# Local and global attention with two feed-forward layers: the scheduler's durations, priorities and engines

## The chip, the cores and the metric

The kernel runs on one core of one Trainium2 chip. The metric is device time in microseconds (us). The kernel before took 911.58 us, the median of three runs (911.21 to 911.71).

The core has engines that run side by side, each with a queue of its own that it works off in order: TensorE (PE) multiplies matrices into PSUM; VectorE (DVE), ScalarE (ACT) and GpSimd (POOL) work element by element; SyncE (SP) issues all DMAs of this kernel. An engine waits at the head of its queue until what the next instruction needs is there, and nothing behind it may overtake.

## The reference

```python
# 4 batches, 8 heads, 512 local and 32 global tokens, head size 64
out_g = softmax(q_g @ k_all.T / 8) @ v_all          # global queries see all 544 keys
s_ll  = where(|i - j| <= 32, q_l @ k_l.T / 8, -1e9) # local queries see a window ...
s_lg  = q_l @ k_g.T / 8                             # ... and the 32 global keys
out_l = softmax([s_lg, s_ll]) @ [v_g, v_l]
x = [out_g, out_l] as 2176 tokens x 512
x = relu(x @ w1_in)**2 @ w1_out                     # 512 -> 2048 -> 512
return relu(x @ w2_in)**2 @ w2_out
```

## The kernel before

**Precision.** Every product of the layers and of the local scores is made of three matmuls: an operand is split into a rounded part (`xh`, `whi`, `gh`, `hk`, `hq`) and the rest (`xl`, `wlo`, `gl`, `lk`, `lq`), and high x high, low x high and high x low are summed in PSUM. So beside each copy that rounds there is a subtraction that makes the rest. The weights come as 64-bit numbers and are put together by four DVE instructions and a sign mask (L466 to L478), then split (L484, `minus("wl", ...)`).

**Attention.** 32 pairs of heads (8 units of 256 local queries, 4 pairs each) go through `pair`: load rk, rq, v; copy and subtract into hk, lk, hq, lq; 12 matmuls of scores into the two banks S0 and S1 (L314); the mask is added and the row minimum taken on DVE (L326); exp on ACT (L331); the sums' reciprocal on DVE (L336, L337); a multiplication of the scores `s` by it (`copy("nm", ...)`); transposes on PE (L349), a copy to `pt`, the product with v into O (L362), and the split of the result into xh (`copy("xh", ...)`) and xl (L373). Eight groups of global queries go through `glob` in the same way between the pairs.

**Layers.** The 2176 token columns are split into five blocks of 256, 512, 512, 512 and 384. Each layer is run in four waves of 512 hidden units; for each block a wave makes h (L509 to L511), on ACT r and gh (L519, L521), on DVE gf (L523), gl by `minus("gl", ...)`, and the product with the second weights (L534 to L536), added to y. A wave needs eight weight tiles: four for h, four for the product. There are 16 slots for them. Slots 8 to 15 lie over the attention's buffers, so weights 8 to 15 can be split only when the attention has ended; weights 0 to 7, of the first wave, come before. The first wave is worked off between the attention's instructions, as its blocks' columns become ready.

**What sets the order.** A planner at build time: every step is an `Op` with an engine, a duration and a priority. `Plan.order` simulates the engines: each takes, of the steps whose inputs are ready, the one with the lowest priority number. The order that comes out is written into the queues. So the durations in the `add` calls and the numbers in `CFG` decide which instruction stands where, and they are not known to the chip. The strings in `CFG` say in turn which engine makes a copy or subtraction (A, D, P for ACT, DVE, POOL): `ck` and `cq` copy hk and hq, `lo` is the subtraction lk, `nm` the multiplication of s, `ev` the copies pt, `xh` the copies xh, `wl` and `gl` the subtractions wlo and gl, `wa` the sign mask of a weight (L473 on DVE, L476 on ACT). `lead`, `lid` and `lmk` are priorities of loads, `glob` the places of the global groups, `moe`, `step`, `w0` and `w1` priorities of the first wave and of its weights.

Of the kernel before, what the change touches and what calls it, by code (L numbers as in the profile page):

```python
# [16 lines left out]
B, H, SL, SG, D = 4, 8, 512, 32, 64  # L17
# [6 lines left out]
WIN = 224  # L24
# [6 lines left out]
WAVES = 4  # L31
NSLOT = 16
CFG = {'EARLY': 8,
 'ck': 'AP',
 'cq': 'PDPD',
 'lo': 'PP',
 'nm': 'PPAD',
 'ev': 'AA',
 'yc': 'AA',
 'wl': 'PPDP',  # L40
 'gl': 'DDP',
 'xh': 'AAAA',
 'glob': [3, 11, 13, 17, 23, 27, 37, 39],
 'w0': 127.954,
 'w1': 1000.0,
 'moe': [122.595, 27.399, 55.448, 83.234, 128.881],
 'step': [0.2, 0.47, 0.409, 0.419, 0.141],
 'NK': 3,
 'NQ': 3,
 'wa': 'DDD',  # L50
 'lid': -23.363,
 'lmk': -11.49,
 'gbuf': '01',
 'lead': 30.038,
 'NM': 2,
 'NS': 3,
 'NPT': 4,
 'NV': 2,
 'NR': 2,
 'NG': 2,  # L60
# [121 lines left out]
def pe_r(n, m=128):  # L182
    return max(n + 32, 2 * m + 6) / 2400
# [3 lines left out]
def kernel(ctx: ExitStack, tc: tile.TileContext, kl, ql, vl, gk, gv, win, wout, msk, idn, out):  # L187
# [97 lines left out]
    def pair(j, prio):  # L285
        u, h2 = divmod(j, H // 2)
        kb, qb, mb, vb = j % NK, j % NQ, j % NM, j % NV
        A = ("arena",)
        q = [prio]

        def P():
            q[0] += 1e-3
            return q[0]

        K, Q, M, ML, HQ, LQ = ("rk", kb), ("rq", qb), ("hk", mb), ("lk", mb), ("hq", mb), ("lq", mb)
        lead = CFG["lead"]
        load(prio - lead, rk[kb], kl[j], 196608, A, (K,))
        load(prio - lead, rq[qb], ql[j], 131072, A, (Q,))
        load(prio - lead + 0.5, vt[vb], vl[j], 229376, A, (("v", vb),))
        copy("ck", P(), hk[mb], rk[kb], KW, A + (K,), (M,))  # L300
        copy("cq", P(), hq[mb], rq[qb], 256, A + (Q,), (HQ,), scalar=-0.125)
        add("DVE", dve(256), P(), lambda: nc.vector.scalar_tensor_tensor(
            out=lq[mb], in0=rq[qb], scalar=-0.125, in1=hq[mb].bitcast(F32),
            op0=ALU.mult, op1=ALU.subtract), A + (Q, HQ), (LQ,), lock=True)
        minus("lo", P(), lk[mb], rk[kb], hk[mb].bitcast(F32), KW, A + (K, M), (ML,))
        sk = [take("S", CFG["S"]) for _ in range(2)]

        def scores():
            for t in range(2):
                c, w = slice(128 * t, 128 * t + 128), slice(160 * t, 160 * t + WIN)  # L310
                for n, (a, b) in enumerate(((hq, hk), (lq, hk), (hq, lk))):
                    for e in range(2):
                        r = slice(64 * e, 64 * e + 64)
                        nc.tensor.matmul(out=bank[sk[e]][:, t * WIN:(t + 1) * WIN], lhsT=a[mb][r, c], rhs=b[mb][r, w],  # L314
                                         start=n == 0, stop=n == 2)

        add("PE", 12 * pe_r(WIN), P(), scores, A + (M, ML, HQ, LQ), tuple(sk))
        pbs = []
        ok = CFG["O"][j % len(CFG["O"])]
        for e in range(2):  # L320
# [13 lines left out]

            def tiny(sb=sb):
                nc.vector.tensor_scalar_add(out=sm[sb], in0=sm[sb], scalar1=1e-9)  # L336
                nc.vector.reciprocal(out=sm[sb], in_=sm[sb])  # L337

            add("DVE", 0.3, P(), tiny, A, (("sm", sb, 0), ("sm", sb, 1)), lock=True)
            for t in range(2):  # L340
                copy("nm", P(), st[sb][:, t, :], st[sb][:, t, :], WIN, A + (("sm", sb, t),), (("s", sb, t),),
                     scalar=sm[sb][:, t:t + 1])
            tk = take("PT", CFG["PT"])

            def trans(sb=sb, tk=tk):
                for t in range(2):
                    for c in range(2):
                        k = 2 * t + c
                        nc.tensor.transpose(bank[tk][0:112, 128 * k:128 * k + 128],  # L349
                                            st[sb][:, t, 112 * c:112 * c + 112], ident)  # L350

            add("PE", 0.44, P(), trans, A + (("s", sb, 0), ("s", sb, 1), "ident"), (tk,))
            pb = i % NPT
            copy("ev", P(), pt[pb][0:112, :], bank[tk][0:112, :], 512, A + (tk,), (("pt", pb),), psum=True)
            pbs.append(pb)

        def pv():
            for t in range(2):
                for c in range(2):
                    k = 2 * t + c  # L360
                    for e in range(2):
                        nc.tensor.matmul(out=bank[ok][64 * e:64 * e + 64, 128 * t:128 * t + 128],  # L362
                                         lhsT=vt[vb][:, 128 * k + 64 * e:128 * k + 64 * e + 64],
                                         rhs=pt[pbs[e]][0:112, 128 * k:128 * k + 128], start=c == 0, stop=c == 1)

        add("PE", 1.2, P(), pv, A + (("pt", pbs[0]), ("pt", pbs[1]), ("v", vb)), (ok,))
        b, c0 = UNIT_POS[u]
        split_out(b, [h2], xh[b][:, h2, c0:c0 + 256], xl[b][:, h2, c0:c0 + 256], ok, bank[ok][:, 0:256], 256, P)

# [7 lines left out]
    def glob(n, prio):  # L377
# [16 lines left out]
        for e in range(2):  # L394
# [4 lines left out]
                    nc.tensor.matmul(out=bank[sk][:, 0:272], lhsT=k[:, 1088 + 128 * pr:1216 + 128 * pr],  # L399
                                     rhs=k[:, S * pr + 272 * e:S * pr + 272 * e + 272], start=pr == 0, stop=pr == 1)  # L400

            add("PE", 0.92, P(), scores, A + (GK,), (sk,))
            add("DVE", 0.37, P(), lambda sk=sk, e=e: nc.vector.tensor_tensor_reduce(
                out=p[:, 272 * e:272 * e + 272], in0=bank[sk][:, 0:272], in1=zeros, op0=ALU.add, op1=ALU.max,
                scale=1.0, scalar=-3.0e38, accum_out=gmx[:, e:e + 1]), A + (sk, "masks"), (GP, "gmx"))
# [279 lines left out]
```

## Time and profile before

| | |
|---|---|
| median of three runs | 911.58 us |
| profiled execution | 911.63 us |
| its span, first to last instruction | 909.2 us |
| PE busy | 890.0 us (98%) |
| DVE busy | 570.4 us (63%) |
| ACT busy | 381.5 us (42%) |
| POOL busy | 214.9 us (24%) |
| mean granted TensorE clock | 0.998 of full |

The engines' shares are means over two very different parts. Up to about 203 us the attention runs, with the first wave's matmuls between; behind that PE has only the layers. Records of two matmuls overlap in time, since the engine starts one before the other has left it, and those of DVE and ACT do so a little; "busy" is the time that at least one record covers.

### The profile page before, as it was taken

How to read it: one execution, taken by the hardware profiler on the slowest of the kernel's cores; microseconds unless marked ns; L12 is line 12 of the kernel's file. 1: busy time of each engine (PE TensorE's matmuls, PEld its weight loads, DVE VectorE, ACT ScalarE, POOL GpSimd, SP SyncE). 2: the span in 40 equal slices, each digit the busy share in tenths (PEclk: the TensorE clock that was granted, in tenths of full speed). 3: DMA queues.
4: the chain of work that ended last, by engine and by line, in shares of the span. 5: the costliest groups of instructions: out<-in, count | busy, mean ns of one | idle time of the engine just before them, and what ended most of it. 6: DMA issues, size and time to landing. Idle time of an engine off the chain costs nothing.

```text
span 909.2 us, 14449 instructions
## 1 busy us (share of the span) xinstructions
PE 890.0 (98%) x5416; PEld 769.1 (85%) x5416; DVE 570.4 (63%) x1311; ACT 381.5 (42%) x885; POOL 214.9 (24%) x241
## 2 busy tenths in 40 slices
PE   5999999999999999999999999999999999999998
PEld 4778777778888988898889988998899889988888
DVE  5888999666557866755786686336754773333333
ACT  5887879683333322223333434343312332122221
POOL 4654556232112122202211221012111120010100
PEclk9999999999999999999999999999999999999999
DMA  8676644212221212200211022102210210001111
GB/s 293 202 239 214 212 133 145 76 31 65 75 70 56 78 53 70 70 24 18 75 50 45 1 70 70 47 1 70 69 47 1 70 47 1 1 1 47 47 47 58
DMA packets 28069, 67.92 MB, mean 75 GB/s; under 512 B 3168, under 2 KB 12512, under 8 KB 28000
## 3 DMA queue, kind: packets, MB, share of 16 engines
q1 hardware_dynamic: 28000, 67.01, 23.1%
q8 instruction: 42, 0.69, 0.3%
q14 instruction: 27, 0.22, 0.1%
HBM read 62.54 MB, written 4.46 MB: 74 GB/s over the span
## 4 chain that ended last, share of the span: by engine, by line
PE 90%; DVE 5%; ACT 2%; DMA 1%; issue 1%; SPq 0%; POOL 0%; DVEq 0%; POOLq 0%; ACTq 0%
PE h L509 8%; PE h L511 7%; PE h L510 7%; PE S L511 6%; PE S L509 6%; PE S L510 6%; PE PT L536 6%; PE PT L534 6%; PE PT L535 6%; PE Y L534 4%; PE Y L536 4%; PE Y L535 4%; PE O L534 3%; PE O L536 3%; PE O L535 3%; PE O L362 2%
## 5 line engine op out<-in xcount | busy, mean ns | idle before, releaser
L221 POOL TENSOR_TENSOR gl<-gf,gh 128x512 fp32r<-128x512 f32 (+2 forms) x53 | 63.1, 1191 | 377.0 <-DVE gf L523 326.9
L519 ACT ACTIVATE r<-h 128x512 f32<-128x512 f32 (+2 forms) x88 | 47.0, 534 | 227.7 <-PE h L511 213.9
L509 PE MATMUL h<-xh,whi 128*128 128x512 f32 (+2 forms) x352 | 129.5, 368 | 1.2 <-DVE gf L523 1.1
L511 PE MATMUL h<-xh,wlo 128*128 128x512 f32 (+2 forms) x352 | 126.4, 359 | 0.9 <-POOL wlo L221 0.9
L510 PE MATMUL h<-xl,whi 128*128 128x512 f32 (+2 forms) x352 | 126.4, 359 | 0.0
L221 POOL TENSOR_TENSOR wlo<-wt,whi 128x512 fp32r<-128x512 f32 x48 | 63.9, 1332 | 217.6 <-ACT whi L484 217.6
L511 PE MATMUL S<-xh,wlo 128*128 128x512 f32 (+2 forms) x288 | 102.8, 357 | 0.0
L510 PE MATMUL S<-xl,whi 128*128 128x512 f32 (+2 forms) x288 | 102.8, 357 | 0.0
L534 PE MATMUL PT<-gh,whi 128*128 128x512 f32 (+2 forms) x288 | 102.8, 357 | 0.0
L509 PE MATMUL S<-xh,whi 128*128 128x512 f32 (+2 forms) x288 | 102.8, 357 | 0.0
L536 PE MATMUL PT<-gh,wlo 128*128 128x512 f32 (+2 forms) x288 | 102.7, 357 | 0.0
L535 PE MATMUL PT<-gl,whi 128*128 128x512 f32 (+2 forms) x288 | 102.7, 357 | 0.0
L521 ACT ACTIVATE gh<-r 128x512 fp32r<-128x512 f32 (+2 forms) x160 | 90.7, 567 | 19.2 <-PE O L536 10.4
L523 DVE SCALAR_TENSOR_TENSOR gf<-h,r 128x512 f32<-128x512 f32 (+2 forms) x88 | 53.5, 608 | 71.6 <-ACT r L519 71.1
L466 DVE TENSOR_SCALAR wt<-wraw 128x512 uint32<-128x512 uint32 x64 | 31.2, 488 | 77.5 <-DMA wraw<-wout 38.8
L484 ACT ACTIVATE whi<-wt 128x512 fp32r<-128x512 f32 x64 | 40.1, 628 | 90.5 <-DVE wt L478 90.5
L534 PE MATMUL Y<-gh,whi 128*128 128x512 f32 (+2 forms) x208 | 76.3, 367 | 0.0
L509 PEld LDWEIGHTS h<-xh,whi 128*128 128x128 f32 x352 | 66.7, 189 | 10.8 <-DVE gf L523 1.6
L523 DVE SCALAR_TENSOR_TENSOR gf<-S,r 128x512 f32<-128x512 f32 (+2 forms) x72 | 43.7, 606 | 50.7 <-ACT r L519 50.4
L536 PE MATMUL Y<-gh,wlo 128*128 128x512 f32 (+2 forms) x208 | 74.9, 360 | 0.3 <-DVE sm L336 0.3
L535 PE MATMUL Y<-gl,whi 128*128 128x512 f32 (+2 forms) x208 | 74.7, 359 | 0.0
L511 PEld LDWEIGHTS h<-xh,wlo 128*128 128x128 f32 x352 | 66.5, 189 | 9.6 <-POOL wlo L221 1.1
(81 smaller groups left out, 1886.5 us busy)
## 6 DMA issues: line engine op xcount, KB each, us to landing
wraw<-win SPq DMA_DIRECT2D x32, 512.0 KB, 3.6
wraw<-wout SPq DMA_DIRECT2D x32, 512.0 KB, 3.5
v<-vl SPq DMA_DIRECT2D x32, 224.0 KB, 3.3
rk<-kl SPq DMA_DIRECT2D x32, 192.0 KB, 3.2
y<-gk SPq DMA_DIRECT2D x8, 672.0 KB, 4.2
y<-gv SPq DMA_DIRECT2D x8, 640.0 KB, 6.1
rq<-ql SPq DMA_DIRECT2D x32, 128.0 KB, 2.9
out<-y SPq DMA_DIRECT2D x12, 256.0 KB, 2.4
```

The source lines that it names most:

```text
L221: add("Pool", 0.25 + 0.0021 * n, prio, lambda: nc.gpsimd.tensor_tensor(out=get(out_), in0=a, in1=get(b), op=ALU.subtract), reads, writes)
L466: add("DVE", dve(512, True), P(), lambda: nc.vector.tensor_scalar(out=t, in0=high, scalar1=3, scalar2=0x3FFFFFF8, op0=ALU.logical_shift_le ...
L484: nc.scalar.activation(out=whi[slot], in_=tf, func=AF.Copy)
L509: nc.tensor.matmul(out=hp, lhsT=hi, rhs=xh[b][:, k, :], start=k == 0, stop=False)
L510: nc.tensor.matmul(out=hp, lhsT=hi, rhs=xl[b][:, k, :], start=False, stop=False)
L511: nc.tensor.matmul(out=hp, lhsT=lo, rhs=xh[b][:, k, :], start=False, stop=k == KD - 1)
L519: add("Activation", act(nb), P(), lambda r=r, hp=hp: nc.scalar.activation(out=r, in_=hp, func=AF.Relu), (hk,), (("r", ri),))
L521: add("Activation", act(nb) + 0.04, P(), lambda r=r, a=a: nc.scalar.activation(out=a, in_=r, func=AF.Square), (("r", ri),), (("gh", f),))
L523: add("DVE", dve(nb), P(), lambda r=r, hp=hp, gf=gf: nc.vector.scalar_tensor_tensor(out=gf, in0=hp, scalar=0.0, in1=r, op0=ALU.max, op1=AL ...
L534: nc.tensor.matmul(out=o, lhsT=hi, rhs=gh[f][:, 0:nb], start=f == 0, stop=False)
L535: nc.tensor.matmul(out=o, lhsT=hi, rhs=gl[f][:, 0:nb], start=False, stop=False)
L536: nc.tensor.matmul(out=o, lhsT=lo, rhs=gh[f][:, 0:nb], start=False, stop=f == 3)
```

## The change

New durations for six kinds of PE steps in the `add` calls; new engines for copies, subtractions, multiplications and sign masks; new priorities and places; one more buffer `pt` (five, not four). No instruction's shape changes and no matmul is added or removed.

```diff
- 'ck': 'AP',
- 'cq': 'PDPD',
- 'lo': 'PP',
- 'nm': 'PPAD',
+ 'ck': 'PPP',
+ 'cq': 'P',
+ 'lo': 'D',
+ 'nm': 'AD',
...
- 'wl': 'PPDP',
- 'gl': 'DDP',
- 'xh': 'AAAA',
- 'glob': [3, 11, 13, 17, 23, 27, 37, 39],
+ 'wl': 'DDPP',
+ 'gl': 'D',
+ 'xh': 'AADA',
+ 'glob': [5, 5, 13, 17, 19, 27, 31, 37],
...
- 'wa': 'DDD',
- 'lid': -23.363,
+ 'wa': 'DAA',
+ 'lid': -317.614,
...
- 'lead': 30.038,
+ 'lead': 14.017,
...
- 'NPT': 4,
+ 'NPT': 5,
...
-        add("PE", 12 * pe_r(WIN), P(), scores, A + (M, ML, HQ, LQ), tuple(sk))
+        add("PE", 0.86, P(), scores, A + (M, ML, HQ, LQ), tuple(sk))
...
-            add("PE", 0.44, P(), trans, A + (("s", sb, 0), ("s", sb, 1), "ident"), (tk,))
+            add("PE", 0.468, P(), trans, A + (("s", sb, 0), ("s", sb, 1), "ident"), (tk,))
...
-        add("PE", 1.2, P(), pv, A + (("pt", pbs[0]), ("pt", pbs[1]), ("v", vb)), (ok,))
+        add("PE", 1.03, P(), pv, A + (("pt", pbs[0]), ("pt", pbs[1]), ("v", vb)), (ok,))
```

(`12 * pe_r(WIN)` is 1.28. The other three durations are of the global groups and change by up to 0.04.)

The SP queue at its start, before (rk, rq and v are one pair's keys, queries and values, ident the unit matrix of the transposes, masks the mask table):

```order
L678 UNCONDITIONAL_BRANCH
L282 DMA rk0_110<-kl 128x384
L282 DMA rq0_113<-ql 128x256
L282 DMA v0_131<-vl 112x512
L282 DMA rk1_111<-kl 128x384
L282 DMA rq1_114<-ql 128x256
L282 DMA v1_132<-vl 112x512
L282 DMA rk2_112<-kl 128x384
L282 DMA rq2_115<-ql 128x256
L282 DMA ident_142<-idn 128x128
L282 DMA masks_141<-msk 128x672
```

The same queue at its start now:

```order
L678 UNCONDITIONAL_BRANCH
L282 DMA ident_143<-idn 128x128
L282 DMA rk0_110<-kl 128x384
L282 DMA rq0_113<-ql 128x256
L282 DMA v0_132<-vl 112x512
L282 DMA rk1_111<-kl 128x384
L282 DMA rq1_114<-ql 128x256
L282 DMA v1_133<-vl 112x512
L282 DMA masks_142<-msk 128x672
```

Ident moved from ninth to first place, the masks from tenth to eighth, and the third pair's rk and rq behind them.

The POOL queue from the third pair on, before (hk and hq are copies, lk a subtraction, s a multiplication):

```order
L211 TENSOR_SCALAR hq0_120<-rq2_115 128x256
L221 TENSOR_TENSOR lk0_118<-rk2_112,hk0_116 128x384
L211 TENSOR_SCALAR s0_124<-s0_124,sm0_136 128x224 x2
L211 TENSOR_SCALAR hk1_117<-rk0_110 128x384
L221 TENSOR_TENSOR lk1_119<-rk0_110,hk1_117 128x384
L211 TENSOR_SCALAR s2_126<-s2_126,sm2_138 128x224 x2
```

The POOL queue from the third pair on now:

```order
L211 TENSOR_SCALAR hk0_116<-rk2_112 128x384
L211 TENSOR_SCALAR hq0_120<-rq2_115 128x256
L211 TENSOR_SCALAR hk1_117<-rk0_110 128x384
L211 TENSOR_SCALAR hq1_121<-rq0_113 128x256
L211 TENSOR_SCALAR hk0_116<-rk1_111 128x384
L211 TENSOR_SCALAR hq0_120<-rq1_114 128x256
```

The subtractions lk and the multiplications s have left POOL; all copies hk and hq are there.

The DVE queue from lq of pair 8 (the ninth) on, before (L403 is a global group's row maximum):

```order
L302 SCALAR_TENSOR_TENSOR lq0_122<-rq2_115,hq0_120 128x256
L336 TENSOR_SCALAR sm0_136<-sm0_136 128x2
L337 RECIPROCAL sm0_136<-sm0_136 128x2
L523 SCALAR_TENSOR_TENSOR gf0_89<-h0_143,r0_87 128x256
L373 TENSOR_TENSOR xl1_70<-O0_150,xh1_65 128x256
L336 TENSOR_SCALAR sm1_137<-sm1_137 128x2
L337 RECIPROCAL sm1_137<-sm1_137 128x2
L403 ISA y3_77,gmx_139<-S0_146,masks_141 128x272
L403 ISA gmx_139 128x1
L208 TENSOR_SCALAR s1_125<-s1_125,sm1_137 128x224
```

The DVE queue from lq of the same pair on now:

```order
L302 SCALAR_TENSOR_TENSOR lq0_122<-rq2_115,hq0_120 128x256
L218 TENSOR_TENSOR lk0_118<-rk2_112,hk0_116 128x384
L336 TENSOR_SCALAR sm0_137<-sm0_137 128x2
L337 RECIPROCAL sm0_137<-sm0_137 128x2
L403 ISA y3_77,gmx_140<-S0_147,masks_142 128x272
L403 ISA gmx_140 128x1
L208 TENSOR_SCALAR s0_124<-s0_124,sm0_137 128x224
L336 TENSOR_SCALAR sm1_138<-sm1_138 128x2
L337 RECIPROCAL sm1_138<-sm1_138 128x2
L403 ISA y3_77,gmx_140<-S1_148,masks_142 128x272
L403 ISA gmx_140 128x1
L208 TENSOR_SCALAR s1_125<-s1_125,sm1_138 128x224
```

The subtraction lk now stands behind lq on DVE, and each of the pair's two heads has one multiplication of s there; before, a pair had one in all.

## Rows read from the trace of the kernel before

**Rows 1.** The page's part 1: engine, busy time, share, instructions.

```profile
span 909.2 us, 14449 instructions
PE 890.0 (98%) x5416; PEld 769.1 (85%) x5416; DVE 570.4 (63%) x1311; ACT 381.5 (42%) x885; POOL 214.9 (24%) x241
```

**Rows 2.** Busy time by stretches: PE, PEld, DVE, ACT, POOL; clock, DMA share, GB/s.

```profile
0.00:9.77 9.77, 1.97 (x12) 1.43 (x12) 2.60 (x3) 2.33 (x3) 4.34 (x10) 1.00 0.80 239
9.77:162.00 152.23, 144.37 (x1484) 116.85 (x1485) 135.43 (x535) 126.02 (x388) 82.50 (x119) 0.99 0.62 200
20.00:40.00 20.00, 17.71 (x201) 13.70 (x198) 18.39 (x78) 16.87 (x56) 12.73 (x18) 1.00 0.64 206
...
120.00:140.00 20.00, 18.73 (x229) 14.77 (x227) 19.25 (x76) 16.41 (x51) 11.34 (x15) 1.00 0.43 131
140.00:160.00 20.00, 18.33 (x173) 15.27 (x173) 18.68 (x67) 18.31 (x55) 12.21 (x17) 1.00 0.45 140
162.00:202.70 40.70, 40.70 (x329) 32.13 (x327) 24.97 (x102) 31.06 (x89) 13.63 (x22) 1.00 0.20 58
202.70:905.60 702.90, 702.90 (x3596) 618.65 (x3594) 406.81 (x671) 222.12 (x405) 114.39 (x92) 1.00 0.15 46
```

**Rows 3.** Timeline of PE in the steady part: start, duration, engine, line, instruction.

```profile
241.05 0.39 PE L509 MATMUL h<-xh,whi 128*128 128x512 f32 x1
241.28 0.39 PE L510 MATMUL h<-xl,whi 128*128 128x512 f32 x1
```

**Rows 4.** Timeline of DVE and POOL near the start.

```profile
3.92 1.00 POOL L221 TENSOR_TENSOR lk<-rk,hk 128x384 fp32r<-128x384 f32 x1
3.99 1.21 DVE L302 SCALAR_TENSOR_TENSOR lq<-rq,hq 128x256 fp32r<-128x256 f32 x1 [3.99 <-POOL hq L211]
...
9.77 0.39 DVE L326 CUSTOM_DVE_ANT_0 s<-S,masks 128x224 f32<-128x224 f32 x1 [1.66 <-DMA masks<-msk]
...
11.02 0.42 DVE L302 SCALAR_TENSOR_TENSOR lq<-rq,hq 128x256 fp32r<-128x256 f32 x1
...
11.36 0.16 DVE L336 TENSOR_SCALAR sm<-sm 128x2 f32<-128x2 f32 x1
...
12.61 0.34 DVE L208 TENSOR_SCALAR s<-s,sm 128x224 f32<-128x224 f32 x1
...
27.24 1.29 POOL L211 TENSOR_SCALAR s<-s,sm 128x224 f32<-128x224 f32 x2 [0.39 <-DVE sm L337]
...
27.34 0.62 DVE L302 SCALAR_TENSOR_TENSOR lq<-rq,hq 128x256 fp32r<-128x256 f32 x1
```

**Rows 5.** Timeline of pair 24's product and of its low part on DVE.

```profile
159.42 1.09 PE L362 MATMUL O<-pt,v 112*64 112x128 f32 x16
...
161.55 0.42 DVE L373 TENSOR_TENSOR xl<-O,xh 128x256 fp32r<-128x256 f32 x1
```

**Rows 6.** Groups by line: count, busy us, mean ns, idle before and releasers.

```profile
L221 POOL TENSOR_TENSOR lk<-rk,hk 128x384 fp32r<-128x384 f32 x32 | 33.9, 1060 | 2.1 <-ACT hk L203 1.0
L211 POOL TENSOR_SCALAR s<-s,sm 128x224 f32<-128x224 f32 x64 | 33.0, 528 | 37.3 <-DVE sm L337 13.7 <-ACT s L331 11.5 <-ACT pt L203 11.5
L302 DVE SCALAR_TENSOR_TENSOR lq<-rq,hq 128x256 fp32r<-128x256 f32 x32 | 19.6, 619 | 4.0 <-POOL hq L211 4.0
L336 DVE TENSOR_SCALAR sm<-sm 128x2 f32<-128x2 f32 x64 | 15.2, 237 | 8.9 <-ACT s L331 8.3
L208 DVE TENSOR_SCALAR s<-s,sm 128x224 f32<-128x224 f32 x32 | 14.9, 464 | 0.2
L218 DVE TENSOR_TENSOR gl<-gf,gh 128x384 fp32r<-128x384 f32 x21 | 11.7, 557 | 2.3 <-ACT gh L521 0.4
L208 DVE TENSOR_SCALAR hq<-rq 128x256 fp32r<-128x256 f32 x16 | 9.1, 571 | 1.5 <-DMA rq<-ql 1.5
```

**Rows 7.** Timeline of DVE: last step (L478) of weights 10 and 15.

```profile
208.50 0.69 DVE L478 SCALAR_TENSOR_TENSOR wt<-wraw,wt 128x512 f32<-128x512 f32 x1
...
244.35 0.69 DVE L478 SCALAR_TENSOR_TENSOR wt<-wraw,wt 128x512 f32<-128x512 f32 x1
```

More of the change, by code (lines that the diff above doesn't have):

```diff
@@ L33 @@
 CFG = {'EARLY': 8,
- 'ck': 'AP',
- 'cq': 'PDPD',
- 'lo': 'PP',
- 'nm': 'PPAD',
- 'ev': 'AA',
- 'yc': 'AA',
- 'wl': 'PPDP',
- 'gl': 'DDP',
- 'xh': 'AAAA',
- 'glob': [3, 11, 13, 17, 23, 27, 37, 39],
[L44 to L47, printed above, removed]
+ 'ck': 'PPP',
+ 'cq': 'P',
+ 'lo': 'D',
+ 'nm': 'AD',
+ 'ev': 'A',
+ 'yc': 'AA',
+ 'wl': 'DDPP',
+ 'gl': 'D',
+ 'xh': 'AADA',
+ 'glob': [5, 5, 13, 17, 19, 27, 31, 37],
+ 'w0': -1.361,
+ 'w1': 684422.049,
+ 'moe': [341.089, 23.225, 54.691, -112.195, -211.616],
+ 'step': [0.2638, 0.5671, 0.1425, 0.013, 0.2305],
  'NK': 3,
  'NQ': 3,
- 'wa': 'DDD',
- 'lid': -23.363,
+ 'wa': 'DAA',
+ 'lid': -317.614,
  'lmk': -11.49,
  'gbuf': '01',
- 'lead': 30.038,
+ 'lead': 14.017,
  'NM': 2,
  'NS': 3,
- 'NPT': 4,
+ 'NPT': 5,
  'NV': 2,
@@ L400, in scores @@
                                      rhs=k[:, S * pr + 272 * e:S * pr + 272 * e + 272], start=pr == 0, stop=pr == 1)
-            add("PE", 0.92, P(), scores, A + (GK,), (sk,))
+            add("PE", 0.96, P(), scores, A + (GK,), (sk,))
             add("DVE", 0.37, P(), lambda sk=sk, e=e: nc.vector.tensor_tensor_reduce(
@@ L425, in trans @@
                 nc.tensor.transpose(bank[t1][:, 128 * c:128 * c + 128], p[:, 128 * c:128 * c + 128], ident)
-        add("PE", 0.44, P(), trans, A + (GP, "ident"), (t1,))
+        add("PE", 0.49, P(), trans, A + (GP, "ident"), (t1,))
         copy("ev", P(), kt[:, 0:512], bank[t1], 512, A + (t1,), (GK,), psum=True)
-        add("PE", 0.11, P(), lambda: nc.tensor.transpose(bank[t2][0:32, 0:128], p[:, 512:544], ident),
+        add("PE", 0.15, P(), lambda: nc.tensor.transpose(bank[t2][0:32, 0:128], p[:, 512:544], ident),
             A + (GP, "ident"), (t2,))
@@ L441, in pv @@
                             rhs=kt[0:kc, 128 * c + 32 * j:128 * c + 32 * j + 32], start=c == 0, stop=c == 4)
-        add("PE", 1.61, P(), pv, A + (GK, GV), (ok,))
+        add("PE", 1.645, P(), pv, A + (GK, GV), (ok,))
         c0 = 256 + 32 * bb
```

## The prediction

> **What bounds the kernel now.** I read first the page's head: of a span of 909.2 us the TensorE (PE) counts as busy in 890.0 [rows 1]. So at most 19.2 us of idle shows, which makes the next question where it lies. The table by stretches answers [rows 2]: from 202.7 us, where the attention's last matmul has ended, to 905.6 PE is busy in 702.90 of 702.9 us, and behind that comes only the 3.6 us in which the last columns are added and stored. All visible idle but that lies before 162 us, 7.8 us up to 9.77 and 7.9 between 9.77 and 162; from 162 to 202.7 PE shows none.
>
> "Busy" hides more. In the steady part a 128x512 matmul is recorded with 0.39 us while the next one starts 0.23 us later [rows 3]; records overlap, so a matmul that is 0.15 us late leaves no idle in the table. The steady part has no such lateness (its matmuls follow each other at 0.23), and a new order can give nothing there: VectorE (DVE) is busy in 406.8 of its 702.9 us. What it can change is the first 202.7 us.
>
> There the reader should look at DVE. In the stretches in which PE shows idle, 20 to 40, 120 to 140 and 140 to 160, DVE is busy 18.39, 19.25 and 18.68 us of 20, a mean of 93.9%; over 9.77 to 162 it is 135.43 of 152.23, or 89.0% [rows 2]. ScalarE (ACT) has 126.0 and GpSimd (POOL) 82.5 in the same 152. So DVE comes last where PE falls back, with ACT close by.
>
> DVE itself waits for POOL inside its records. At 3.92 POOL begins a subtraction of 1.00 us, and the DVE instruction that begins at 3.99 takes 1.21; the same instruction with POOL idle takes 0.42 [rows 4]. A short POOL instruction holds it less: beside the two multiplications from 27.24 on it takes 0.62.
>
> And the first 9.77 us are a wait for the mask table: the first mask instruction on DVE starts there, released by that DMA, and scores of the next pair wait for it [rows 4].
>
> **The change part by part.** *The planner's durations* (scores 1.28 to 0.86 us of plan time, transposes, products) move no time by themselves: the matmuls are the same ones, and the chip doesn't know the plan. All effect comes through the new order and the new engines.
>
> *The start.* The SP queue now issues ident first and the masks eighth instead of tenth. Ahead of the masks stand 1.18 MB instead of 1.51 MB. At the 239 GB/s of the first 9.77 us [rows 2] the 0.33 MB are worth 1.4 us; in a queue with nothing else to do it could be as little as nothing, if the masks' own transfer sets the time. I take 1.1 us: masks at 8.7 in place of 9.77. The first pair's chunks arrive one issue later, which costs nothing as long as the masks come after its scores.
>
> *DVE's ledger up to the low part of pair 24's output* (L373; the 25th of 32 pairs, and the place where before has its worst stretch behind it). Counted in the program order of both, with durations less the overlap of 0.08 that records there show (one of 0.42 whose successor starts 0.34 later) [rows 4]:
> 28 subtractions lk come from POOL, at 0.48 each by the 0.557 of DVE's other 128x384 subtraction [rows 6]: +13.4. 27 more multiplications of s, at 0.34 - 0.08 [rows 4]: +7.0. 14 copies hq go to POOL, at the same price: -3.6. Eight copies xh from PSUM, five of 256 columns at 0.34 and three small ones: +2.1. Three more 128x512 subtractions at 0.64 and one of 256 columns: +2.3. One gf more: +0.6. Five sign masks L473 go to ACT: -1.7. Two more weight instructions stand ahead of this place: +1.3. Sum +21.4 us.
>
> *Against that, what POOL no longer holds.* The means of DVE's records against the unheld ones [rows 4] give what POOL costs it now: L302 (619 - 420 ns) x 32 = 6.4 us, L208 s (464 - 340) x 32 = 4.0, L336 (237 - 160) x 64 = 4.9, L208 hq (571 - 340) x 16 = 3.7 [rows 6]; 19.0 over 32 pairs, so 15 up to pair 24. POOL loses 28 subtractions of 1.06 us and 52 multiplications of 0.53, and gains 28 copies of about half a microsecond: its busy time up to there falls from 82.5 to some 39 us. In proportion DVE would still be held for 7 us; as what is left is short, and long ones hold longer, I take 5 (ends: 2, and 15 if nothing gets better). Relief 10 us.
>
> DVE's busy time to that place becomes 135.4 + 21.4 - 10 = 146.8 us. *ACT* gets 27 multiplications and six sign-masks and loses 14 hk and 8 xh copies: 11 instructions at its mean of 0.32 us, +4 on 126 of 152; it doesn't become the bound.
>
> *What PE gets for it.* Up to the product O of pair 24 the attention matmuls are the same in both orders, but after has 36 more 128x512 matmuls of the first layer ahead of it: at 0.227 [rows 3] 8.2 us of work already done. Before, that product ends at 159.42 + 1.09 = 160.5, and xl, its low part on DVE, 1.5 us later [rows 5].
>
> The step that decides is how full DVE is. I take the mean of the three stretches in which it came last, 93.9%: PE had reserve there and DVE none, and with the longer ledger DVE should come last nearly throughout. Then 146.8 / 0.939 = 156.4; from the masks at 8.7 that ends at 165.1, the product 1.5 earlier at 163.6. Before would have needed until 160.5 + 8.2 = 168.7 for as much work. Gain 5.1 us. At 89.0%, the mean over the whole stretch, the same sum ends 3.4 us later than before; at the best stretch's 96.3% it gains 9.0.
>
> *Behind pair 24* seven pairs are left in either order, where PE is full in 162 to 202.7 [rows 2]; I take no gain and no loss, with 2 us to either side. *The weights at the end of the attention* lose cover: weights 8 to 15 are written over the attention's buffers, so they start when its last product is done. In before the first matmul of weight 10 follows 44.5 us of PE work later, that of weight 15 77.8; in after 29.8 and 47.5. Weights 10 to 15 are finished on DVE at intervals of (244.35 - 208.50) / 5 = 7.2 us [rows 7], and weight 10's low part is there 8 us after the last product. So 15 is ready at 8 + 5 x 7.2 = 44, 3.5 us before it is needed. Hidden; the cover is used up when the interval grows by 0.7 us, to 7.9, and what it grows beyond that PE waits five times over.
>
> *The steady part*: DVE takes over 53 subtractions gl from POOL and gives two of three L473 to ACT. DVE at 58% covers it.
>
> The profiled execution took 911.63 us, its span and 2.4 around it, within 0.1 of the median of the three timed ones. 911.63 - 5.1 = 906.5.
>
> **The rivals.** *DVE is no better packed than now.* At 89.0% the attention reaches the same point 3.4 us later: 915.0. It decides from 90.9% downward, where 146.8 us take 161.5, as long as before. For it: outside the three stretches DVE was busy (135.43 - 56.32) / (152.23 - 60) = 86% and PE still came late now and then, so both can wait for each other in chains, while the queues run in order; more of a pair's chain (lk, then lq, the masks, the sums, half the multiplications) now sits in one queue. Against it: where PE waited for DVE it was over 91% each time, and two hops to POOL leave each pair's chain.
>
> *POOL holds DVE nearly as before.* The two multiplications at 27.24 held the DVE instruction as well, 0.62 against 0.42 [rows 4], so short copies do hold; and DVE runs more instructions that can be held. Of these (subtractions, multiplications, L302 and the weight chain in SBUF) after has about 1.3 times as many up to pair 24. 15 x 39 / 82.5 x 1.3 = 9 us of holding stay; DVE has 151 us, 160.9 at 93.9%, and the gain shrinks to 0.7: 910.9. The Trainium skill, "GPSIMD Engine Reference", Key points, has the rule: GpSimd's SBUF interfaces are VectorE's too, and it contends with DVE instructions that have two SBUF inputs or run in a 2-port mode. By it every lk and s that moves to DVE is one more that can be held; rows 4 agree in kind. The rule gives no price, and the sum of my forecast stands without it.
>
> *DVE is packed as in its best stretch*, since its queue nearly always holds ready work: 96.3%, 902.6; with holding at its lower end of 2 us 900.
>
> **How the numbers follow.** Forecast 906.5 with 0.42, its own range 903 to 909.5; better packed 0.25; held nearly as before 0.13; no better packed 0.20. The first two are faster by over 0.2%, that is 1.8 us, about what a measurement of this kernel can tell from no change: 0.67. Held is within it: 0.13. The last is slower: 0.20. The range goes from 899.5, the best packing with the low end of holding and half a microsecond, to 915, the no-better-packed case; the end without any relief (15 us of holding: 917) is left out.
>
> **What would show it.** Right: the first mask instruction at about 8.7; POOL busy near 40 us up to pair 24; L302's mean near 0.45; xl of pair 24 ending near 165 with DVE at 93% or more since the masks; the attention's last product, with 23.5 us more of the first layer ahead of it, ending near 202.7 + 23.5 - 5 = 221; 0.23 from matmul to matmul behind it. Wrong: xl of pair 24 at 170 or later with DVE under 90%, or with L302 still near 0.6; or PE idle behind the last product before weights 14 and 15.

## The result, and the profile after

The changed kernel took 904.38 us, the median of 4 runs (903.92 to 904.77), against 911.64 us for the kernel before beside it (4 runs, 911.21 to 913.55): a ratio of 0.9916 [0.9899, 0.9933]. It is faster by 7.3 us. The forecast was 906.5, faster, with a range of 899.5 to 915.

The page's head of the kernel after answers to [rows 1]. The profiled execution took 904.31 us, 1.8 of them around the span:

```profile
span 902.5 us, 14362 instructions
PE 888.0 (98%) x5416; PEld 765.8 (85%) x5416; DVE 577.3 (64%) x1396; ACT 405.2 (45%) x933; POOL 80.7 (9%) x108
```

POOL's 214.9 us have shrunk to 80.7; DVE's total has grown by 6.9 us only, though it runs 85 instructions more. The table by stretches, with the columns of [rows 2], cut at the first mask instruction, at the low part of pair 24 and at the attention's last product:

```profile
0.00:9.12 9.12, 1.96 (x12) 1.43 (x12) 2.06 (x4) 1.28 (x1) 2.38 (x8) 1.00 0.75 211
9.12:162.80 153.68, 149.81 (x1517) 120.97 (x1518) 142.91 (x586) 131.37 (x404) 36.78 (x64) 1.00 0.65 204
20.00:40.00 20.00, 19.83 (x236) 16.49 (x235) 19.10 (x85) 17.75 (x55) 5.08 (x8) 1.00 0.76 238
...
60.00:80.00 20.00, 19.87 (x236) 15.86 (x235) 19.12 (x85) 16.38 (x53) 6.44 (x11) 1.00 0.76 237
...
120.00:140.00 20.00, 19.16 (x219) 16.45 (x219) 17.62 (x75) 17.11 (x55) 5.84 (x10) 1.00 0.48 146
140.00:160.00 20.00, 19.28 (x154) 15.19 (x154) 18.85 (x69) 17.41 (x52) 2.96 (x6) 1.00 0.37 108
...
162.80:219.70 56.90, 56.90 (x404) 45.20 (x402) 29.31 (x114) 35.95 (x98) 3.55 (x8) 1.00 0.12 31
219.70:898.90 679.20, 679.20 (x3488) 598.22 (x3486) 402.52 (x693) 236.65 (x431) 38.04 (x28) 1.00 0.15 48
```

Where the kernel before had PE busy for 17.71, 18.73 and 18.33 us of 20 [rows 2], it is now busy for 19.83, 19.16 and 19.28. Behind the attention nothing has changed in kind: 679.20 busy of 679.20.

Busy time hides lateness, so I also took each matmul's start to the next start, less the usual step of its kind, and added these up. The numbers are how late PE is at a time, in us:

| at | 20 us | 40 | 80 | 120 | 160 | 220 | 890 |
|---|---|---|---|---|---|---|---|
| before | 12.9 | 17.6 | 22.7 | 24.8 | 31.7 | 34.2 | 34.9 |
| after | 14.8 | 15.7 | 18.9 | 21.3 | 24.9 | 27.6 | 28.2 |

The difference at the end is the span's 6.7 us. It is made between 20 and 40 us (4.7 lost before, 0.9 now), between 40 and 80 (5.1 and 3.2) and between 120 and 160 (6.9 and 3.6). In the second of these before loses some 1.7 us from 64 to 67.5 us at the lower of TensorE's two clock levels (the rows are in the last section):

```profile
60.00:80.00 20.00, 18.37 (x181) 15.39 (x182) 16.57 (x70) 15.00 (x46) 10.22 (x14) 0.91 0.70 222
```

The columns are those above; the mean granted clock is 0.91 here and 1.00 in the same stretch after. It isn't this execution alone: of the 70 runs of before beside the experiments, 53 have a mean granted clock of 0.998 or less over the whole run (median 912.2 us) and 17 have 0.999 or 1.0 (median 910.2), while all four runs of after have 0.999 or 1.0. So some 1.7 to 2 of the 7.3 us go with the clock.

The groups by line of the kernel after (count, busy us, mean ns, idle before) answer to [rows 6]:

```profile
L208 DVE TENSOR_SCALAR s<-s,sm 128x224 f32<-128x224 f32 x64 | 22.4, 351 | 0.4
L218 DVE TENSOR_TENSOR lk<-rk,hk 128x384 fp32r<-128x384 f32 x32 | 18.0, 563 | 6.5 <-POOL hk L211 6.5
L302 DVE SCALAR_TENSOR_TENSOR lq<-rq,hq 128x256 fp32r<-128x256 f32 x32 | 14.9, 466 | 0.5 <-POOL hq L211 0.5
L336 DVE TENSOR_SCALAR sm<-sm 128x2 f32<-128x2 f32 x64 | 13.2, 207 | 3.4 <-ACT s L331 3.0
```

The same instructions are shorter: L302 466 ns for 619, the multiplication L208 351 for 464, L336 207 for 237.

### The profile page after: what moved, and what is told of

Same layout as the page of the kernel before. It is cut to its first block, busy times and chain, and to the rows that moved or that the text cites. A ratio compares the mean times of both kernels' runs of the same rounds, so it can differ in the third digit from the quotient of the medians.

```text
span 902.5 us, 14362 instructions
## 1 busy us (share of the span) xinstructions
PE 888.0 (98%) x5416; PEld 765.8 (85%) x5416; DVE 577.3 (64%) x1396; ACT 405.2 (45%) x933; POOL 80.7 (9%) x108
## 4 chain that ended last, share of the span: by engine, by line
PE 92%; DVE 4%; ACT 2%; DMA 2%; issue 0%; SPq 0%; ACTq 0%
PE h L509 8%; PE h L510 7%; PE h L511 7%; PE S L510 6%; PE S L509 6%; PE S L511 6%; PE PT L534 6%; PE PT L536 6%; PE PT L535 6%; PE Y L534 5%; PE Y L536 4%; PE Y L535 4%; PE O L534 3%; PE O L535 3%; PE O L536 3%; PE O L362 3%
## 5 line engine op out<-in xcount | busy, mean ns | idle before, releaser
L218 DVE TENSOR_TENSOR gl<-gf,gh 128x512 fp32r<-128x512 f32 (+2 forms) x160 | 99.5, 623 | 21.5 <-ACT gh L521 10.4
L536 PE MATMUL PT<-gh,wlo 128*128 128x512 f32 (+2 forms) x288 | 102.6, 356 | 0.0
L535 PE MATMUL PT<-gl,whi 128*128 128x512 f32 (+2 forms) x288 | 102.6, 356 | 0.0
L221 POOL TENSOR_TENSOR wlo<-wt,whi 128x512 fp32r<-128x512 f32 x32 | 43.6, 1364 | 521.5 <-ACT whi L484 521.5
L536 PE MATMUL Y<-gh,wlo 128*128 128x512 f32 (+2 forms) x208 | 74.6, 359 | 0.0
L535 PE MATMUL Y<-gl,whi 128*128 128x512 f32 (+2 forms) x208 | 74.6, 359 | 0.0
L510 PEld LDWEIGHTS h<-xl,whi 128*128 128x128 f32 x352 | 66.5, 189 | 7.8 <-DVE xl L373 0.2
L547 DVE TENSOR_TENSOR y<-y,Y 128x512 f32<-128x512 f32 (+2 forms) x30 | 18.2, 606 | 84.3 <-PE Y L536 84.2
L519 ACT ACTIVATE r<-S 128x512 f32<-128x512 f32 (+2 forms) x72 | 38.4, 533 | 67.8 <-PE S L511 65.2
```

What stands on the lines that cost most here:

```text
L218: add("DVE", dve(n), prio, lambda: nc.vector.tensor_tensor(out=get(out_), in0=a, in1=get(b), op=ALU.subtract), reads, writes, lock=True)
L221: add("Pool", 0.25 + 0.0021 * n, prio, lambda: nc.gpsimd.tensor_tensor(out=get(out_), in0=a, in1=get(b), op=ALU.subtract), reads, writes)
L510: nc.tensor.matmul(out=hp, lhsT=hi, rhs=xl[b][:, k, :], start=False, stop=False)
L519: add("Activation", act(nb), P(), lambda r=r, hp=hp: nc.scalar.activation(out=r, in_=hp, func=AF.Relu), (hk,), (("r", ri),))
L535: nc.tensor.matmul(out=o, lhsT=hi, rhs=gl[f][:, 0:nb], start=False, stop=False)
L536: nc.tensor.matmul(out=o, lhsT=lo, rhs=gh[f][:, 0:nb], start=False, stop=f == 3)
```

## The experiments

Two theories were open. The forecast's: DVE is what PE waits for, and it gains because POOL holds it less and the masks come sooner. The rival: no engine's load decides; what counts is what work stands ready in PE's queue while a pair's chain is under way, and that belongs to the whole plan. All times are medians, each beside runs of the kernel before on the same chip (911.46 to 911.92).

**One part of the change at a time.** The change has three parts: the engines, the durations, and the priorities (with the places, the order of loads and the fifth buffer). Five kernels make one or two of them. x1 is before with the new engines alone:

```
- 'ck': 'AP',  'cq': 'PDPD', 'lo': 'PP', 'nm': 'PPAD', 'ev': 'AA', 'wl': 'PPDP', 'gl': 'DDP', 'xh': 'AAAA', 'wa': 'DDD',
+ 'ck': 'PPP', 'cq': 'P',    'lo': 'D',  'nm': 'AD',   'ev': 'A',  'wl': 'DDPP', 'gl': 'D',   'xh': 'AADA', 'wa': 'DAA',
```

> The kernel before with only the engine letters of the change (hk, hq, lk, s, xh, wlo, gl, sign mask); priorities, durations, load order and buffers as before; planned anew. Theory A (the gain comes from what leaves POOL): 904 to 907 us, about the whole gain, L302 near 0.46 us. Theory B (the gain comes from the new priorities, load order and places, the engines are a side matter): 910 to 913. Theory C (DVE's longer queue needs the new priorities to be filled): slower than before, 914 to 920.

912.15 us, 1.0001 [0.9981, 1.002]: no gain. x2 is after with the old engines (the same lines the other way round), so it has the priorities and the durations:

> The changed kernel with only the engine letters of before; new priorities, durations, load order and fifth pt buffer stay; planned anew. Theory A (relief of POOL): 910 to 913 us, the gain is gone. Theory B (order): 903 to 906. If both parts carry some: 906 to 909.

914.51 us, 1.0024 [1.0009, 1.004]. x3 is before with the six new durations of PE's work:

```
- add("PE", 12 * pe_r(WIN), P(), scores, ...
+ add("PE", 0.86, P(), scores, ...
- add("PE", 1.2, P(), pv, ...
+ add("PE", 1.03, P(), pv, ...
... (four more alike)
```

> The kernel before with only the six PE durations of the change; all of CFG as before; planned anew. If the planner's durations carry the gain: 904 to 907 us. If they only reshuffle ties: 910 to 913, within 0.2% of before. My own expectation is the second, since the chip's matmuls don't change and DVE, not PE, came last where time was lost.

918.75 us, 1.008 [1.0061, 1.0098]: slower by 7.0. x7 is after with the old durations, so it has the engines and the priorities:

> The changed kernel with the six PE durations of before; all of CFG as changed; planned anew. If the durations carry the gain: 909 to 912 us. If the engines and priorities carry it whatever the durations: 903.5 to 906. A plan that is wrong by 0.42 us in each of 32 score steps could also misplace matmuls: then 906 to 909.

912.5 us, 1.0003 [0.9989, 1.0017]. So y3 put engines and durations together, into before:

> The kernel before with the new engine letters and the six new durations; priorities, load order, places and buffers as before; planned anew. If engines and durations are the substance and the priorities a side matter: 904 to 907 us. If all three belong together, as the three kernels with one or two parts say (912.2, 914.5, 912.5): 910 to 916.

922.51 us, 1.0109 [1.0085, 1.0134], the slowest of all. Neither the engines nor the durations carry the 7 us by themselves, nor do any two of the three parts; the priorities alone were not run. The clock has a share in the two slowest: x3 has a mean granted clock of 0.994 to 0.996 in nine of its ten runs, and the one at 1.0 took 915.68; y3 has 0.992 to 0.998.

x1 is the telling one, since it has the relief and the load of after. From 20 to 160 us, first x1, then after:

```profile
20.00:160.00 140.00, 131.46 (x1428) 106.89 (x1428) 131.48 (x539) 119.60 (x369) 37.97 (x62) 1.00 0.60 188
```

```profile
20.00:160.00 140.00, 137.62 (x1442) 111.33 (x1441) 131.40 (x543) 121.72 (x374) 33.94 (x58) 1.00 0.62 190
```

DVE is equally busy in both, 131.5 and 131.4 us, with 539 and 543 instructions, and its L302 takes 420 ns in x1:

```profile
L302 DVE SCALAR_TENSOR_TENSOR lq<-rq,hq 128x256 fp32r<-128x256 f32 x32 | 13.4, 420 | 0.3 <-POOL hq L211 0.3
```

PE differs by 6.2 us. The product of pair 24 begins at 160.8 us in x1 and at 160.9 in after; what differs is how much of the layers' work PE has done ahead of it. For all kernels with all of PE's work, with that part counted in the program's order at the usual steps (the places are those of the profiled execution, the medians those of all runs):

| kernel | product of pair 24 at | layers' work ahead | first less second | median us |
|---|---|---|---|---|
| before | 159.4 | 24.4 | 135.0 | 911.6 |
| after | 160.9 | 32.6 | 128.3 | 904.4 |
| x1: engines | 160.8 | 23.8 | 137.0 | 912.2 |
| x2: priorities, durations | 171.0 | 31.9 | 139.1 | 914.5 |
| x3: durations | 157.6 | 17.7 | 139.9 | 918.8 |
| x7: engines, priorities | 161.2 | 26.1 | 135.1 | 912.5 |
| y3: engines, durations | 157.3 | 17.4 | 140.0 | 922.5 |
| x4 (below) | 166.3 | 32.6 | 133.7 | 908.8 |
| x5 (below) | 163.5 | 24.4 | 139.1 | 915.3 |
| y1 (below) | 154.6 | 20.6 | 134.0 | 912.6 |
| y2 (below) | 171.7 | 35.3 | 136.4 | 910.9 |
| x6 (below) | 162.1 | 32.6 | 129.5 | 905.1 |
| x8 (below) | 161.2 | 32.6 | 128.6 | 903.8 |

The attention's own work ahead of that place is the same in all, but for one more pair's scores (0.86 us) in x1, x3, x7, y1 and y3. So the difference of the two columns says how late PE is there, whatever made it late: it adds up the loss and doesn't explain it. The count of the layers' work alone says little: x2 and y2 have 31.9 and 35.3 us of it ahead and still are no faster than before, since their pair 24 comes 10 us later than that of after.

**Holding by POOL, at an unchanged order.** x4 keeps the order of after and has only the subtraction lk done by POOL, in DVE's place in the plan:

```
- add("DVE", dve(n), prio, lambda: nc.vector.tensor_tensor(
+ eng = nc.gpsimd if key == "lo" else nc.vector
+ add("DVE", dve(n), prio, lambda: eng.tensor_tensor(
```

> The changed kernel with its order kept and the 32 subtractions lk issued on POOL in place of DVE (the planner still counts them as DVE's). DVE loses 32 x 0.48 = 15 us of work. Theory H (POOL's subtractions hold DVE): L302 back to 0.55 to 0.65 us, DVE's holding up by 8 to 12 us, and lk comes 0.5 us later in each pair's chain; time 905 to 909, no better than the changed kernel. Theory L (DVE's own load alone sets the pace): 895 to 900.

908.84 us, 0.9969 [0.9953, 0.9984]: 4.5 us more than after, although DVE has 32 subtractions less; that is within the range of theory H. Its busy time from 20 to 160 us, and its groups by line:

```profile
20.00:160.00 140.00, 135.87 (x1414) 109.17 (x1413) 128.35 (x507) 119.44 (x365) 58.74 (x82) 1.00 0.59 185
...
L219 POOL TENSOR_TENSOR lk<-rk,hk 128x384 fp32r<-128x384 f32 x32 | 34.5, 1079 | 0.0
...
L303 DVE SCALAR_TENSOR_TENSOR lq<-rq,hq 128x256 fp32r<-128x256 f32 x32 | 18.4, 575 | 6.7 <-POOL hq L211 6.7
```

L302 (L303 here) is back from 466 to 575 ns, and DVE is still busy for 128.35 us of 140, against 131.40 with the subtractions. POOL's subtraction takes 1079 ns for DVE's 563, so holding and the longer path to the scores are not told apart by this run. x5 does the opposite in before's order, lk on DVE in POOL's place:

```
- add("Pool", 0.25 + 0.0021 * n, prio, lambda: nc.gpsimd.tensor_tensor(
+ eng = nc.vector if key == "lo" else nc.gpsimd
+ add("Pool", 0.25 + 0.0021 * n, prio, lambda: eng.tensor_tensor(
```

> The kernel before with its order kept and the 32 subtractions lk issued on DVE in place of POOL. DVE gets 15 us more, POOL loses 34. Theory H (holding): L302 falls from 0.62 to about 0.47, holding falls by 8 us up to pair 24, and lk is ready earlier; 909 to 912, no change or a little faster. Theory L (DVE's own load alone): 918 to 924.

915.26 us, 1.0032 [1.0013, 1.0051]: slower by 3.8, between the two theories' ranges, with L302 at 445 ns. Part of that goes with the clock: eight of the ten runs have a mean granted clock of 0.996 or less, and the one at 1.0 took 911.74 us, only 1.5 more than the 910.2 of before at 0.999 or 1.0. The swap pays neither way by itself.

**DVE's load by itself.** x8 is after without the addition of 1e-9 to the local sums (L336), 64 instructions of DVE and 13.2 us by the group above; nothing else moves:

```
-                nc.vector.tensor_scalar_add(out=sm[sb], in0=sm[sb], scalar1=1e-9)
```

> The changed kernel with its order kept, without the addition of 1e-9 to the local queries' sums (64 DVE instructions L336 of 0.21 us; the reciprocal then reads the sum as it is). DVE loses about 0.19 us x 64 = 12 us of work, 9.5 up to pair 24, and each pair's chain 0.2 us. Theory L (DVE comes last through most of the attention): 896 to 899 us. If the matmuls' own small losses or ACT set the pace by now, with DVE only close by: 902 to 904.

903.76 us, 0.9912 [0.9878, 0.9945]: 0.6 us less than after, within the two intervals, and far from the 896 to 899 of theory L.

```profile
20.00:160.00 140.00, 138.12 (x1444) 111.95 (x1443) 123.74 (x495) 121.22 (x375) 33.41 (x59) 1.00 0.61 189
```

DVE's busy time falls by 7.7 us of 140, to 88%, and PE's rises by 0.5. How full DVE is doesn't set the time of after, whose PE has little left to gain.

**PE's load by itself.** y4 is after without one of the three products of the local scores (hq with lk), 9.2 us of PE's work by the usual steps:

```
- for n, (a, b) in enumerate(((hq, hk), (lq, hk), (hq, lk))):
+ for n, (a, b) in enumerate(((hq, hk), (lq, hk))):
...
- start=n == 0, stop=n == 2)
+ start=n == 0, stop=n == 1)
```

> The changed kernel with its order kept, leaving out the third of the three products of the local scores (hq x lk; lk is still computed): PE loses 128 matmuls, by the twelve-matmul group of 0.86 us some 0.29 us x 32 = 9.2 us of work, and each pair's chain 0.29 us; DVE, ACT and POOL keep all theirs. Theory PE (in the changed kernel PE itself sets the pace of the attention, start and switches between kinds of matmul apart): 895 to 897 us. Theory DVE (DVE comes last): 902 to 904.5. Balanced: 898 to 901.

900.62 us, 0.9872 [0.9858, 0.9887]: 3.8 us less than after, the balanced case. So PE's own work counts, up to some 4 us, behind which the next limit lies. Each pair's chain gets 0.29 us shorter as well, which this run can't tell apart; that a shorter chain alone does it is unlikely, since x8 takes some 0.2 us out of each and gains 0.6 in all. In the same stretch PE is then busy for less:

```profile
20.00:160.00 140.00, 135.72 (x1369) 107.92 (x1368) 131.53 (x545) 122.81 (x380) 35.63 (x58) 1.00 0.61 193
```

**The masks.** x6 is after with the masks' transfer issued fourth in place of eighth:

```
...
+ sp = [op for op in ops if op.eng == "SP"]
+ table = next(op for op in sp if op.prio == CFG["lmk"])
+ ops.remove(table)
+ ops.insert(ops.index(sp[2]) + 1, table)
...
```

> The changed kernel with its order kept, except that the mask table's DMA is issued fourth in place of eighth, right behind the first pair's keys and queries. If the 3.3 us for which PE stands idle before 9.98 us are the masks' alone: the first mask instruction at 5.5 to 6.5 us, 901 to 902.5 us in all. If what the table is moved past (the second pair's loads) comes late in its place, or if DVE takes the gain back later: 903.5 to 905.

905.05 us, 0.9923 [0.9896, 0.995]: no gain. The timelines of SyncE's queue and of DVE (start, duration, engine, instruction, idle before and its end), of x6 and then of after:

```profile
2.11 0.43 SPq L282 DMA_DIRECT2D masks<-msk  x1
...
8.57 0.56 DVE L218 TENSOR_TENSOR lk<-rk,hk 128x384 fp32r<-128x384 f32 x1 [3.12 <-POOL hk L211]
9.43 0.43 DVE L302 SCALAR_TENSOR_TENSOR lq<-rq,hq 128x256 fp32r<-128x256 f32 x1 [0.30 <-POOL hq L211]
9.77 0.38 DVE L326 CUSTOM_DVE_ANT_0 s<-S,masks 128x224 f32<-128x224 f32 x1
```

```profile
4.00 0.43 SPq L282 DMA_DIRECT2D masks<-msk  x1
...
7.57 0.56 DVE L218 TENSOR_TENSOR lk<-rk,hk 128x384 fp32r<-128x384 f32 x1 [2.05 <-POOL hk L211]
8.43 0.43 DVE L302 SCALAR_TENSOR_TENSOR lq<-rq,hq 128x256 fp32r<-128x256 f32 x1 [0.30 <-POOL hq L211]
9.12 0.39 DVE L326 CUSTOM_DVE_ANT_0 s<-S,masks 128x224 f32<-128x224 f32 x1 [0.27 <-DMA masks<-msk]
```

In DVE's queue lk and lq of the next pair stand ahead of the first mask instruction. With the masks earlier their chunks come 1.0 us later, lk starts at 8.57 for 7.57, and the mask instruction at 9.77 with no wait for its table. Moving lk and lq behind it as well wasn't tried.

**How much of the gain is this one plan.** y1 is after with one number of its planner changed by 2.4% and the order made anew; y2 does the same to before:

```
- add("PE", 1.03, P(), pv, ...
+ add("PE", 1.055, P(), pv, ...
... (y1; y2:)
- add("PE", 1.2, P(), pv, ...
+ add("PE", 1.23, P(), pv, ...
```

> The changed kernel with one planner's duration nudged (the product with v 1.055 in place of 1.03 us, 2.4%); all else as changed; planned anew. Theory J (the gain belongs to one plan that was chosen whole, and any new plan from nearly the same inputs loses most of it): 907 to 913 us. Theory P (right durations make good plans, and a slip of 2% does little): 903.5 to 905.5.

y1: 912.58 us, 1.0006 [0.9992, 1.002]. The whole gain is gone, in the runs at a granted clock of 1.0 as well (912.1 to 912.5).

> The kernel before with the same duration nudged as much (1.23 in place of 1.2 us, 2.5%); all else as before; planned anew. Theory J: the plan of before was chosen whole as well, so a nudge costs it, 913 to 920 us. Theory P (its durations were wrong anyway): 910 to 913, within 0.2% of before.

y2: 910.88 us, 0.999 [0.9975, 1.0004]. Before loses nothing. One nudge of each was tried, so how often a plan breaks is not known.

y1 falls back behind 130 us. Its table by stretches, and then that of after:

```profile
130.00:140.00 10.00, 8.79 (x99) 6.60 (x95) 9.75 (x40) 9.31 (x29) 2.66 (x5) 1.00 0.44 126
140.00:150.00 10.00, 7.66 (x79) 5.89 (x75) 9.46 (x39) 8.90 (x28) 3.19 (x5) 1.00 0.63 188
...
160.00:165.00 5.00, 3.20 (x24) 2.62 (x20) 4.93 (x17) 5.00 (x14) 0.23 (x1) 1.00 0.19 58
165.00:170.00 5.00, 4.70 (x15) 3.34 (x14) 3.72 (x11) 1.77 (x6) 0.00 (x0) 0.66 0.07 11
```

```profile
130.00:140.00 10.00, 10.00 (x120) 8.72 (x119) 9.27 (x43) 9.77 (x32) 1.82 (x4) 1.00 0.54 169
140.00:150.00 10.00, 9.28 (x86) 7.18 (x86) 9.83 (x33) 9.54 (x30) 2.08 (x4) 1.00 0.33 94
```

From 130 to 150 DVE is busy for 19.21 and 19.10 us of 20, ACT for 18.21 and 19.31, PE for 16.45 and 19.28. PE's groups by line from 130 to 165 us (count, busy us, mean ns, idle before) say what it did with that, y1 and then after:

```profile
L349 PE MATMUL PT<-ident,s 128*112 128x128 f32 x52 | 8.2, 284 | 2.4 <-ACT s L203 2.4
...
L534 PE MATMUL Y<-gh,whi 128*128 128x256 f32 x14 | 4.6, 331 | 0.0
```

```profile
L534 PE MATMUL Y<-gh,whi 128*128 128x512 f32 (+1 forms) x21 | 8.2, 391 | 0.0
L349 PE MATMUL PT<-ident,s 128*112 128x128 f32 x52 | 7.5, 277 | 0.0
```

Both make 52 transposes, so the attention goes on at much the same pace. Between them y1 has 14 matmuls with the second weights on this line, all of 256 columns, and after has 21, of which 13 are of 512; L535 and L536 repeat that. With h it is 6.1 us of the layers' work in y1 and 15.1 in after, at the usual steps. As I read it, what y1's queue holds behind its transposes is not enough to fill their waits. Its pair 24 comes at 154.6, 6.3 us before that of after, but with 12.0 us less of the layers ahead of it, and these are then left for when there is nothing more to fill.

No version that computes everything beat the changed kernel.

## Why the prediction was right, and where it was not

The sign and the size came out: 5.1 us forecast, 7.3 measured. That the size came so near is in part luck, since the step that set it, DVE as the engine that comes last, doesn't hold in after. By its steps:

- *The masks.* Forecast at 8.7, the first mask instruction came at 9.12, 0.65 earlier than before and not 1.1. It now waits 0.27 us for its table, behind lk and lq of the next pair, which waited for POOL's hk and hq. PE's next scores follow at 9.98 for 10.63. By 20 us nothing of this is left: PE is 1.9 us later there than before (the table of lateness).
- *DVE's ledger.* 146.8 us of busy time were forecast from the first mask instruction to the low part of pair 24's product; it is 142.91. Taking each DVE record's excess over the shortest tenth of its form, DVE is held for 9.6 us of this stretch where before had 21.7 in its own: a relief of 12.1 for the 10 forecast, the difference of two terms that were both too small (5 and 15). The other 1.8 us lie in the work that DVE takes over: 142.9 - 135.4 + 12.1 = 19.6 for 21.4. POOL's busy time there is 36.8 for the 39 forecast, and L302's 466 ns answer to the 0.45.
- *How full DVE is.* 93.9% was taken and 142.91 / 153.68 = 93.0% measured. xl of pair 24 ends at 162.41 + 0.42 = 162.8 for 165.1, its product at 161.9 for 163.6. The 93.9% itself was lucky: it is the mean of three stretches of 20 us, but before's PE shows idle of over 1 us in a fourth, 60 to 80 (the row above: PE 18.37, DVE 16.57). With that one the mean is 91.1%, 146.8 / 0.911 = 161.1, the product comes at 168.3, and the same sum forecasts a gain of 168.7 - 168.3 = 0.4 us, no change. The rows of pair 24 in after:

```profile
160.85 1.09 PE L362 MATMUL O<-pt,v 112*64 112x128 f32 x16
...
162.41 0.42 DVE L373 TENSOR_TENSOR xl<-O,xh 128x256 fp32r<-128x256 f32 x1 [0.53 <-ACT xh L203]
```

With the 8.2 us of first-layer work ahead of it, that is a gain of 160.5 + 8.2 - 161.9 = 6.8 us. Some 1.7 of it is the loss at the lower clock that after doesn't have; no term of the sum stood for it.
- *Behind pair 24* no gain was taken and none is there: the span's gain is 6.7. The last product ends near 219.7 for the 221 forecast:

```profile
218.66 1.10 PE L362 MATMUL O<-pt,v 112*64 112x128 f32 x16
219.69 0.45 PE L509 MATMUL h<-xh,whi 128*128 128x384 f32 x1
219.97 0.34 PE L510 MATMUL h<-xl,whi 128*128 128x384 f32 x1
```

- *The weights* are hidden, as forecast, but by little: PE shows no idle from there to 898.9. Weights 10 and 15 are finished on DVE at intervals of (264.26 - 225.55) / 5 = 7.7 us, for 7.2 forecast and 7.9 at which the cover is used up:

```profile
225.55 0.68 DVE L478 SCALAR_TENSOR_TENSOR wt<-wraw,wt 128x512 f32<-128x512 f32 x1
...
264.26 0.69 DVE L478 SCALAR_TENSOR_TENSOR wt<-wraw,wt 128x512 f32<-128x512 f32 x1
```

- *Around the span* lie 1.8 us for 2.4. 6.7 + 0.6 = 7.3, the measured gain.

904.4 lies between the forecast and the rival "packed as in its best stretch" (902.6). The rivals at 910.9 and 915.0 are out: the product of pair 24 comes 6.8 us sooner for as much work. The one at 910.9 had the holding that stays about right (9 us, 9.6 measured), nearer than the forecast's 5; it failed because before was held for 21.7 us and not for 15, so that less than half is left.

One step is borne out only in part: "The step that decides is how full DVE is", with DVE coming last nearly throughout. In after it doesn't come last: x8 takes 7.7 us from DVE's 140 and gains 0.6. And a relieved DVE at the same fill gains nothing by itself: x1 has after's DVE load and relief, and its pair 24 comes at the same time, but with 8.8 us less of the layers ahead of it. DVE, with ACT, may well set the attention's pace where PE waits (19.2 of 20 us in y1 from 130 to 150); whether PE loses by it depends, as I read the rows of y1, on the layers' matmuls that stand ready in its queue; that is argued, not shown. Of the two numbers that did the work in my sum, that was the 8.2 us, which I read out of the new order and gave no doubt of its own.

What limits after most is PE's own work. Between 20 and 220 us after is 27.6 - 14.8 = 12.8 us late, and by my weighing 12.5 of this lie in its 203 changes from one kind of matmul to another (below). Before has 34.2 - 12.9 = 21.3 us, of which its 189 changes take 11.6: 9.7 are left for waiting, the 1.7 at the lower clock among them. The 0.3 that is left in after is too little, since an excess at a change is counted as its price up to 0.2 us: PE shows 140 - 137.62 = 2.4 us of idle from 20 to 160, and with the shortest steps in place of the usual ones the waiting is 2.9 us in after and 10.3 in before. y4 agrees: less work for PE shortens after, by 3.8 of 9.2 us.

That holding costs time is supported by x4, with the reserve named there. Not settled: the priorities alone, with the old engines and durations, were not run; no run took work from DVE in the order of before, where it may have been the limit; and that before and x1 fall back for want of layers' work in PE's queue rests on the counts in the table of pair 24, which y1's rows agree with for one stretch, not on a run that moves a few layers' matmuls by hand.

## What to carry to other kernels

An engine that is 93% busy beside the one that bounds the kernel may have nothing left to give: take some work from it at an unchanged order and see (x8), before a sum is built on its fill. In a kernel whose order comes from a planner, parts of a change can't be priced one by one (912.2, 914.5, 918.8, 912.5 and 922.5 us for parts of a change that gave 904.4), and a gain of under 1% may belong to one plan, which one number 2.4% off takes away. The time of a late point less the independent work ahead of it tells how late the bounding engine is there: here the rest of the kernel added 774.5 to 778.9 us to it in all kernels but y3, which loses 4 to 8 us more behind that point (782.5). It needs the measured time of the point; the count of work ahead, which can be read from an order beforehand, was not enough. And look at the granted clock of every run before a small difference is explained: here it went with some 2 us.

## What the runs showed of the hardware

Going from the attention's matmuls to the layers' costs PE about 0.1 us. In before and after together the first matmul of the layers behind attention work is followed 0.08 to 0.11 us later than its usual step in 92 of 95 cases, and 0.20 us later in all seven behind a global group's scores; from h to the product with the second weights or back, it is within 0.01 us of the step in 178 of 180. In the rows of after at 218.66 above, the first 128x384 matmul behind the products O is followed after 0.28 us, the next ones after 0.18 (219.97 to 220.15). The timeline of PE at 101 us, the first layer's matmuls behind a global group's scores, the dearer case, and ahead of a pair's transposes:

```profile
101.23 0.59 PE L509 MATMUL h<-xh,whi 128*128 128x512 f32 x1
101.67 0.40 PE L510 MATMUL h<-xl,whi 128*128 128x512 f32 x1
101.90 0.40 PE L511 MATMUL h<-xh,wlo 128*128 128x512 f32 x1
102.14 0.60 PE L349 MATMUL PT<-ident,s 128*112 128x128 f32 x4
```

The first is followed after 0.44 us, the second after 0.23, the steady step of [rows 3]. With 203 changes of all kinds from 20 us to the last product they are the largest part of what PE still loses there, 12.5 us by the weighing above; what causes it was not tried.

TensorE's clock fell to the lower of its two levels (1.2 of 2.4 GHz) behind pauses of PE inside the attention. Before, by stretches:

```profile
62.00:63.00 1.00, 0.10 (x2) 0.00 (x0) 0.97 (x6) 0.74 (x2) 1.00 (x1) 1.00 0.46 116
63.00:64.00 1.00, 0.37 (x1) 0.18 (x1) 1.00 (x7) 1.00 (x6) 0.78 (x2) 1.00 0.59 104
64.00:65.00 1.00, 0.90 (x8) 0.90 (x10) 0.90 (x6) 1.00 (x5) 0.35 (x1) 0.57 0.99 377
65.00:66.00 1.00, 1.00 (x9) 0.80 (x8) 0.94 (x6) 0.47 (x3) 1.00 (x3) 0.50 1.03 363
```

PE is busy for 0.47 of the 2 us up to 64, and from 65 on the granted clock is 0.50, while PE is busy throughout; y1 has the same in its rows above (3.20 busy of 5, then 0.66). So a wait can be paid for a second time, here with some 1.7 us behind a pause of 1.5; after shows 1.00 in all its stretches up to 898.9.
